# Another order inside the steps that ScalarE and VectorE interleave with a gated projection

## The chip, the cores and the metric

One core of one Trainium2 chip runs the whole program in one launch. The metric is the device time of a run in microseconds (us); lower is better. Three runs of the kernel before gave a median of 799.67 us (799.30 to 800.97).

## The reference

Attention with a window and sinks, then a gated projection, all in float32. There are 4 batches, 8 heads, 768 positions, head size 64. A query sees the first 4 positions (the sinks) and the 128 positions up to its own:

```python
scores = scale * np.matmul(q, k.transpose(0, 1, 3, 2))
keep = is_sink | in_window
scores = np.where(keep, scores, -1000000000.0)
a = softmax(scores)                 # row maximum taken off, 1e-9 added to the sum
x = np.matmul(a, v)                 # heads side by side: 3072 tokens x 512
out = ((x @ w_a) * (x @ w_b)) @ w_out   # 512 -> 1536 -> 512
```

## The kernel before, in words

The 3072 tokens are cut into 8 chunks of 2 to 4 tiles of 128 tokens (`CHUNKS`). `run` computes the projection of chunk c (`moe`) and, between its pieces, the attention of chunk c+1. The projection runs over 12 blocks j. A block is: `half("a", j)`, 12 matmuls into PSUM (L969); one step of attention; `half("b", j)`, 12 matmuls; a step; `project` of the block before, 9 matmuls of 512 columns (L978); a step. The text calls the three steps of a block A, B and O after the piece in front of them. Every product is kept in two rounded parts, high and low (`xh`, `xl`; `gh`, `gl`; hi and lo slots of `pt`).

The change touches the chunks whose attention is `steady`: chunks 3 to 7, computed during the projections of chunks 2 to 6. For those, `run` opens `manual_schedule` for TensorE, VectorE and ScalarE: these three engines execute in the order in which the program emits. GpSimd (POOL) and the DMA queue are ordered by the planner. Chunks 3 and 6 begin at tile 0 of their batch (below: head stages, during the projections of chunks 2 and 5); chunks 4, 5 and 7 begin at tile 3 (below: full stages, during the projections of chunks 3, 4 and 6).

A unit is one head and one tile of queries. `steady_plan` gives every step at most one unit to score, the unit scored two steps before to transpose, and at most one of three other things: `av` (the product of a head's three units with the values, three steps after its last unit), `skt` (transposes of four heads' sink weights) and `sk` (their product, twice). One step in the middle of the plan has no unit to score. In a step the operations are:

- scoring: two matmuls into the single PSUM tile `s` (L617); VectorE merges window edges and sinks (L625), subtracts and takes the maximum (L627); ScalarE exponentiates (L632); VectorE inverts the sum (L635, L636); ScalarE scales the unit (L642) and writes its sinks into `sc` (L645).
- turning a unit that lies wholly in the window ("joined"): a transpose into one half of the PSUM bank `t` (L661); ScalarE rounds it in place and into `p` (L674, L675); VectorE multiplies by a triangle and subtracts (L681, L682, L683) into `pt`, of which there is one.
- `av`: seven matmuls (L697); ScalarE copies one half of the rows (L704), VectorE adds the other (L707, L708).
- `skt`: three transposes into the tile tag `s` (L715); ScalarE rounds (L721), VectorE subtracts (L724), ScalarE copies both parts (L725). `sk`: one matmul (L731), VectorE adds (L733).
- the gate: ScalarE copies the a half to `g` (L988; one buffer); VectorE multiplies by the b half (L994); ScalarE rounds to `gh` (L999); GpSimd subtracts to `gl` (L1001), on VectorE in the last two blocks.

Before the change ScalarE's order in a step was: L988 (emitted in `moe` ahead of step A), L674, L675, L632, then `late_act` (L999, in step B), L704, L642, L645. VectorE's was: L994 (emitted in `moe` ahead of step B), L625, L627, L681 to L683, L635, L636, L707, L708. `between` spreads the steps over the blocks, about one after every piece.

Of the kernel before, what the change touches and what calls it, by code (L numbers as in the profile page):

```python
# [13 lines left out]
ALU = mybir.AluOpType  # L14
# [9 lines left out]
NJ = FF // P  # L24
# [199 lines left out]
class Fast:  # L224
# [367 lines left out]
    def steady(self, b, t0, nt, xf):  # L592
        nc = self.nc
# [6 lines left out]
        units = [(h, i) for h in range(H) for i in range(nt)]  # L600
        preps, state, sc, vss, skt, bank = {}, {}, {}, {}, {}, []

        def do_prep(h):
            if h < H:
                preps[h] = *self.prep_kq(b, h, t0, nt), self.prep_v(b, h, t0, nt)
                if h % 4 == 0:
                    vss[h // 4] = self.vs
# [125 lines left out]
            return (lambda: None), (lambda: V.tensor_tensor(x, ps[:, :cols], x, op=ALU.add))  # L733

        plan = self.steady_plan(units, nt)
        do_prep(0)
        yield
        for score, turn, rest in plan:
            turned = evicted = ()
            scored = ()  # L740
            if score is not None:
                if score[1] == 0:
                    do_prep(score[0] + 1)
                scored = scores(*score)
            if turn is not None:
                turned = transposes(*turn)
            if rest is not None:
                evicted = {"av": av, "skt": sinks_t, "sk": sinks_av}[rest[0]](*rest[1:])
            if turned:
                turned[0]()  # L750
            if scored:
                scored[0]()
                scored[1]()
            if turned:
                turned[1]()
            self.late_act()
            if evicted:
                evicted[0]()
            if scored:
                scored[2]()  # L760
                scored[3]()
            if evicted:
                evicted[1]()
            yield

    def steady_plan(self, units, nt):

        gap = 4 * nt + 1
        at = {}
        for k, u in enumerate(units):  # L770
            at[u] = k + (k >= gap)
        rest = {}
        for h in range(H):
            rest[at[h, nt - 1] + 3] = ("av", h)
        for g in range(2):
            k = at[4 * g + 3, nt - 1] + 2
            rest[k] = ("skt", g)
            for pr in range(2):
                while k in rest or k <= at[4 * g + 3, nt - 1] + 4:
                    k += 1  # L780
                rest[k] = ("sk", g, pr)
        score = {k: u for u, k in at.items()}
        turn = {k + 2: u for u, k in at.items()}
        n = max(*rest, *turn) + 1
        return [(score.get(k), turn.get(k), rest.get(k)) for k in range(n)]
# [169 lines left out]
    def moe(self, row, nt, xf, between, weights_ahead, last, weights_split, given):  # L955
        nc = self.nc
        n = nt * P
        tag = f"{row}"
        xs = self.split_x(xf, nt, tag)
        outs = [self.ps.tile([P, DM], F32, tag=("o0", "o1", "o2", "av")[i], name=f"o{tag}_{i}") for i in range(nt)]  # L960

        def half(kind, j):
            wh, wl = self.weight(kind, j)
            ps = self.ps.tile([P, 4 * P], F32, tag=kind, name=f"{kind}{tag}_{j}")
            for kk in range(NK):
                ksl = slice(kk * P, (kk + 1) * P)
                xh, xl = xs[kk]
                for i, (w, x) in enumerate(((wh, xh), (wh, xl), (wl, xh))):
                    nc.tensor.matmul(ps[:, :n], lhsT=w[:, ksl], rhs=x[:, :n],  # L969
                                     start=kk == 0 and i == 0, stop=kk == NK - 1 and i == 2)  # L970
            return ps

        def project(j, gh, gl):
            wh, wl = self.weight("o", j)
            for i in range(nt):
                sl = slice(i * P, (i + 1) * P)
                for k, (g, w) in enumerate(((gh, wh), (gh, wl), (gl, wh))):
                    nc.tensor.matmul(outs[i], lhsT=g[:, sl], rhs=w,  # L978
                                     start=j == 0 and k == 0, stop=j == NJ - 1 and k == 2)

        prev = None
        for j in range(NJ):
            if last and j == NJ - 2:
                self.ok = self.verdict(self.ps.tile([1, P], F32, tag="s", name="gp"))
            weights_ahead(3 * j)
            pa = half("a", j)
            g = self.mo.tile([P, max(n, 3 * P)], F32, tag="g", name=f"g{tag}_{j}", bufs=1)
            nc.scalar.copy(g[:, :n], pa[:, :n])  # L988
            between(3 * j)
            if last and j == NJ - 1:  # L990
                self.tc.mark_branch_hint_location("general", hint="LikelyTaken", engines=mybir.ALL_ENGINES)
            weights_ahead(3 * j + 1)
            pb = half("b", j)
            nc.vector.tensor_tensor(g[:, :n], pb[:, :n], g[:, :n], op=ALU.mult)  # L994
            gh = self.mo.tile([P, max(n, 3 * P)], F32R, tag="gh", name=f"gh{tag}_{j}")
            gl = self.mo.tile([P, max(n, 3 * P)], F32R, tag="gl", name=f"gl{tag}_{j}")

            def parts(j=j, g=g, gh=gh, gl=gl):
                nc.scalar.copy(gh[:, :n], g[:, :n])  # L999
                e = nc.gpsimd if weights_split and j < NJ - 2 else nc.vector  # L1000
                e.tensor_tensor(gl[:, :n], g[:, :n], gh[:, :n].bitcast(F32), op=ALU.subtract)  # L1001

            self.later.append(parts)
            if not given or j == NJ - 1:
                self.late_act()
            between(3 * j + 1)
            self.late_act()
            weights_ahead(3 * j + 2)
            if prev is not None:
                project(*prev)  # L1010
            between(3 * j + 2)
            prev = (j, gh, gl)
        project(*prev)
        for i in range(nt):
            r = row + i * P
            o = self.mo.tile([P, DM], F32, tag=("gh", "gl")[i % 2], name=f"os{tag}_{i}")
            (nc.vector.tensor_copy if last and i == 1 else nc.scalar.copy)(o, outs[i])
            (nc.sync if last else nc.scalar).dma_start(self.out[r:r + P, :], o)
# [175 lines left out]
```

## Time and profile before

| | |
|---|---|
| median of 3 runs | 799.67 us (799.30 to 800.97) |
| the profiled execution's own time | 800.83 us |
| its span, first to last instruction | 799.1 us |
| TensorE (PE) busy, weight loads (PEld) | 774.2 us (97%), 686.3 us (86%) |
| VectorE (DVE), ScalarE (ACT), GpSimd (POOL) busy | 525.0, 475.4, 292.2 us |
| granted TensorE clock | 0.996 of full speed |

The five steady stages lie between 242 us and 714 us of the span. Busy shares say who has most to do; how much time TensorE loses is read from the starts of its matmuls, because they are pipelined and the recorded end of one lies past the start of the next.

### The profile page before, as it was taken

The page shows a single profiled execution, that of the slowest core. Times are in us where ns is not written, and L with a number is a line of the kernel's source. Part 1 is how long each engine was busy: PE and PEld are TensorE (multiplying, and loading weights), DVE is VectorE, ACT ScalarE, POOL GpSimd, SP SyncE. Part 2 cuts the span into 40 slices and gives each one's busy share as a digit, 9 for nine tenths or more (in the row PEclk, how much of TensorE's full clock was granted, in tenths as well). Part 3 has the DMA queues.
Part 4 walks back from the last instruction along what each step waited for, and adds up shares of the span by engine and source line. Part 5 has one row for each costly group of instructions (what it writes and reads, how often), then busy time and mean ns, then how long its engine had stood idle before and what let it go on. Part 6 is the DMA issues. An engine that isn't in the chain of part 4 may idle for free.

```text
span 799.1 us, 13885 instructions
## 1 busy us (share of the span) xinstructions
PE 774.2 (97%) x4349; PEld 686.3 (86%) x4349; DVE 525.0 (66%) x1759; ACT 475.4 (59%) x1485; POOL 292.2 (37%) x400
## 2 busy tenths in 40 slices
PE   8999999989999999999999999999999999999997
PEld 5768777779799989998989889899998988889996
DVE  6888889977773767367873777636675487742321
ACT  5867577737755767366653666547774566644431
POOL 1110000146642655355660657406545375201110
PEclk9999999999999999999999999999999999999999
DMA  8777400242121332412111111212333121105511
GB/s 318 272 268 274 180 17 1 74 140 57 50 75 41 103 117 91 140 30 62 46 57 50 45 44 48 57 40 90 119 114 101 53 65 40 41 17 186 177 57 43
DMA packets 44574, 75.85 MB, mean 95 GB/s; under 512 B 4592, under 2 KB 24016, under 8 KB 44496
## 3 DMA queue, kind: packets, MB, share of 16 engines
q1 hardware_dynamic: 41440, 69.40, 27.0%
q10 hardware_dynamic: 3024, 5.51, 1.8%
q8 instruction: 36, 0.59, 0.3%
q14 instruction: 42, 0.34, 0.1%
q0 software_dynamic: 32, 0.00, 0.0%
HBM read 68.60 MB, written 6.29 MB: 94 GB/s over the span
## 4 chain that ended last, share of the span: by engine, by line
PE 59%; DVE 23%; ACT 10%; issue 3%; POOL 2%; DMA 2%; ACTq 0%; DVEq 0%; POOLq 0%
PE a L969 16%; PE o L978 16%; PE b L969 14%; DVE pt L681 3%; DVE pt L683 3%; DVE t L682 2%; PE av L697 2%; PE s L831 2%; PE s L617 2%; ACT p L675 2%; ACT g L988 1%; PE av L885 1%; ACT p L642 1%; DVE st L636 1%; ACT sc L645 1%
## 5 line engine op out<-in xcount | busy, mean ns | idle before, releaser
L969 PE MATMUL a<-xh,w 128*128 128x384 f32 (+2 forms) x768 | 214.2, 342 | 0.8 <-ACT w L353 0.8
L969 PE MATMUL b<-xh,w 128*128 128x384 f32 (+2 forms) x768 | 213.9, 342 | 0.0
L978 PE MATMUL o<-w,gh 128*128 128x512 f32 x576 | 185.3, 402 | 1.0 <-ACT gh L999 1.0
L969 PEld LDWEIGHTS a<-xh,w 128*128 128x128 f32 x768 | 138.5, 188 | 5.9 <-ACT w L353 1.1
L969 PEld LDWEIGHTS b<-xh,w 128*128 128x128 f32 x768 | 138.8, 188 | 4.1 <-issue 0.3
L1001 POOL TENSOR_TENSOR gl<-g,gh 128x384 fp32r<-128x384 f32 x60 | 60.9, 1016 | 217.1 <-ACT gh L999 212.3
L969 PE MATMUL b<-xl,w 128*128 128x384 f32 (+2 forms) x384 | 129.3, 337 | 0.0
L969 PE MATMUL a<-xl,w 128*128 128x384 f32 (+2 forms) x384 | 129.0, 336 | 0.0
L994 DVE TENSOR_TENSOR g<-b,g 128x384 f32<-128x384 f32 (+2 forms) x96 | 53.2, 554 | 106.9 <-PE b L969 95.2
L978 PEld LDWEIGHTS o<-w,gh 128*128 128x128 f32 x576 | 103.5, 189 | 20.3 <-ACT gh L999 1.7
L978 PE MATMUL o<-w,gl 128*128 128x512 f32 x288 | 114.1, 397 | 0.4 <-DVE gl L1001 0.4
L988 ACT COPY g<-a 128x384 f32<-128x384 f32 (+2 forms) x96 | 45.5, 474 | 75.4 <-PE a L969 63.9
L969 PEld LDWEIGHTS a<-xl,w 128*128 128x128 f32 x384 | 72.3, 188 | 2.4
L969 PEld LDWEIGHTS b<-xl,w 128*128 128x128 f32 x384 | 72.4, 189 | 1.6
L999 ACT CAST gh<-g 128x384 fp32r<-128x384 f32 (+2 forms) x96 | 48.6, 506 | 36.4 <-DVE g L994 34.7
L642 ACT ACTIVATE p<-p,st 128x128 f32<-128x128 f32 x88 | 35.6, 405 | 58.2 <-DVE st L636 57.7
L387 POOL TENSOR_SCALAR ks<-kr 64x400 fp32r<-64x400 f32 (+1 forms) x48 | 29.0, 605 | 107.4 <-DVE pt L548 105.5
L632 ACT ACTIVATE p<-p,st 128x136 f32<-128x136 f32 (+2 forms) x120 | 51.2, 426 | 26.0 <-DVE st L627 24.5
L978 PEld LDWEIGHTS o<-w,gl 128*128 128x128 f32 x288 | 54.1, 188 | 14.3 <-DVE gl L1001 1.7
L390 POOL TENSOR_TENSOR ks<-kr,ks 64x400 fp32r<-64x400 f32 (+1 forms) x48 | 58.0, 1208 | 3.8
L681 DVE TENSOR_TENSOR pt<-t,tri 128x256 fp32r<-128x256 f32 x88 | 37.3, 424 | 33.0 <-ACT p L675 30.3
L387 POOL TENSOR_SCALAR qh<-qr 128x384 fp32r<-128x384 f32 x48 | 25.1, 523 | 69.7 <-PE s L617 41.0
(192 smaller groups left out, 1437.1 us busy)
## 6 DMA issues: line engine op xcount, KB each, us to landing
qr<-in_qT_dram SPq DMA_DIRECT2D x48, 192.0 KB, 2.4
raw<-in_wa_dram SPq DMA_DIRECT2D x12, 512.0 KB, 6.6
raw<-in_wb_dram SPq DMA_DIRECT2D x12, 512.0 KB, 6.9
raw<-in_wo_dram SPq DMA_DIRECT2D x12, 512.0 KB, 7.2
chk_a<-in_wa_dram SPq DMA_DIRECT2D x24, 256.0 KB, 2.9
chk_b<-in_wb_dram SPq DMA_DIRECT2D x24, 256.0 KB, 2.8
chk_o<-in_wo_dram SPq DMA_DIRECT2D x24, 256.0 KB, 2.8
out_dram<-os ACTq DMA_DIRECT2D x21, 256.0 KB, 2.0
```

Source lines behind the costliest of these rows:

```text
L387: self.nc.gpsimd.tensor_scalar(o, i, 1.0, 1.0, op0=ALU.mult, op1=ALU.mult)
L390: (self.nc.vector if self.no_gpsimd else self.nc.gpsimd).tensor_tensor(o, i, high.bitcast(F32), op=ALU.subtract)
L632: A.activation(p[:, :n], p[:, :n], AF.Exp, bias=st[:, 0:1], scale=-1.0, accum_out=st[:, 1:2])
L642: A.mul(p[:, NS:KB], p[:, NS:KB], st[:, 3:4])
L681: V.tensor_tensor(hs, tp[:, 1:2, :].broadcast_to([P, 2, P]), tri, op=ALU.mult)
L683: V.tensor_tensor(ls, tp[:, 0:1, :].broadcast_to([P, 2, P]), tri, op=ALU.mult)
L969: nc.tensor.matmul(ps[:, :n], lhsT=w[:, ksl], rhs=x[:, :n], start=kk == 0 and i == 0, stop=kk == NK - 1 and i == 2)
L978: nc.tensor.matmul(outs[i], lhsT=g[:, sl], rhs=w, start=j == 0 and k == 0, stop=j == NJ - 1 and k == 2)
L988: nc.scalar.copy(g[:, :n], pa[:, :n])
L994: nc.vector.tensor_tensor(g[:, :n], pb[:, :n], g[:, :n], op=ALU.mult)
L999: nc.scalar.copy(gh[:, :n], g[:, :n])
L1001: e.tensor_tensor(gl[:, :n], g[:, :n], gh[:, :n].bitcast(F32), op=ALU.subtract)
```

## The change

In `steady`: the sinks' transposes and their reading (L715, L721, L724, L725) come first in their step; ScalarE rounds the transposed unit before it exponentiates, as before, but `av`'s copy and add now come before the scaling; the unit scaled (L642, L645) is the one scored a step earlier; the inverse comes after; `late_act` comes last. In `moe`, the copy L988 becomes part of `late_act`, and so does the product L994, ahead of L999. In `steady_plan`, the `sk` products may follow the last `av` directly at the end, so the plan has 30 steps in place of 31, and `between` leaves out one more place (after the projection in block 5); all later steps of the plan come one place later, and the last one falls in the same place as before.

```diff
--- before.py
+++ after.py
@@ -733,35 +733,43 @@
             return (lambda: None), (lambda: V.tensor_tensor(x, ps[:, :cols], x, op=ALU.add))
 
         plan = self.steady_plan(units, nt)
+        pending = lambda: None
         do_prep(0)
         yield
         for score, turn, rest in plan:
-            turned = evicted = ()
-            scored = ()
+            turned = evicted = scored = ()
+            sinks = rest is not None and rest[0] == "skt"
             if score is not None:
                 if score[1] == 0:
                     do_prep(score[0] + 1)
                 scored = scores(*score)
+            if sinks:
+                evicted = sinks_t(rest[1])
+                evicted[0]()
+                evicted[1]()
             if turn is not None:
                 turned = transposes(*turn)
-            if rest is not None:
-                evicted = {"av": av, "skt": sinks_t, "sk": sinks_av}[rest[0]](*rest[1:])
+            if rest is not None and not sinks:
+                evicted = {"av": av, "sk": sinks_av}[rest[0]](*rest[1:])
+            if scored:
+                scored[0]()
             if turned:
                 turned[0]()
             if scored:
-                scored[0]()
                 scored[1]()
             if turned:
                 turned[1]()
-            self.late_act()
-            if evicted:
+            if evicted and not sinks:
                 evicted[0]()
+                evicted[1]()
+            pending()
+            pending = lambda: None
             if scored:
                 scored[2]()
-                scored[3]()
-            if evicted:
-                evicted[1]()
+                pending = scored[3]
+            self.late_act()
             yield
+        pending()
 
     def steady_plan(self, units, nt):
 
@@ -776,7 +784,7 @@
             k = at[4 * g + 3, nt - 1] + 2
             rest[k] = ("skt", g)
             for pr in range(2):
-                while k in rest or k <= at[4 * g + 3, nt - 1] + 4:
+                while k in rest or k - 1 in rest and rest[k - 1][0] == "av" and k + 1 < len(units):
                     k += 1
                 rest[k] = ("sk", g, pr)
         score = {k: u for u, k in at.items()}
@@ -985,17 +993,20 @@
             weights_ahead(3 * j)
             pa = half("a", j)
             g = self.mo.tile([P, max(n, 3 * P)], F32, tag="g", name=f"g{tag}_{j}", bufs=1)
-            nc.scalar.copy(g[:, :n], pa[:, :n])
+            self.later.append(lambda g=g, pa=pa: nc.scalar.copy(g[:, :n], pa[:, :n]))
+            if not given or j == NJ - 1:
+                self.late_act()
             between(3 * j)
+            self.late_act()
             if last and j == NJ - 1:
                 self.tc.mark_branch_hint_location("general", hint="LikelyTaken", engines=mybir.ALL_ENGINES)
             weights_ahead(3 * j + 1)
             pb = half("b", j)
-            nc.vector.tensor_tensor(g[:, :n], pb[:, :n], g[:, :n], op=ALU.mult)
             gh = self.mo.tile([P, max(n, 3 * P)], F32R, tag="gh", name=f"gh{tag}_{j}")
             gl = self.mo.tile([P, max(n, 3 * P)], F32R, tag="gl", name=f"gl{tag}_{j}")
 
-            def parts(j=j, g=g, gh=gh, gl=gl):
+            def parts(j=j, g=g, gh=gh, gl=gl, pb=pb):
+                nc.vector.tensor_tensor(g[:, :n], pb[:, :n], g[:, :n], op=ALU.mult)
                 nc.scalar.copy(gh[:, :n], g[:, :n])
                 e = nc.gpsimd if weights_split and j < NJ - 2 else nc.vector
                 e.tensor_tensor(gl[:, :n], g[:, :n], gh[:, :n].bitcast(F32), op=ALU.subtract)
```

## Rows read from the trace of the kernel before

**Rows 1.** Busy time of each engine in the five steady stages, in order (the stage of 242.3 and that of 525.5 are the head stages): the stretch in us, its length, then busy us and count of instructions of PE, PEld, DVE, ACT, POOL; PEclk, DMA share, GB/s.
```profile
242.30:332.10 89.80, 89.18 (x516) 83.21 (x516) 54.23 (x203) 57.23 (x192) 45.56 (x62) 1.00 0.32 100
332.10:429.00 96.90, 94.33 (x536) 86.55 (x535) 65.06 (x234) 55.61 (x188) 49.05 (x62) 1.00 0.17 51
429.00:525.50 96.50, 93.93 (x534) 86.17 (x533) 64.67 (x232) 55.22 (x188) 47.88 (x62) 1.00 0.17 48
525.50:617.00 91.50, 90.77 (x524) 84.55 (x523) 54.41 (x204) 58.09 (x192) 45.52 (x62) 1.00 0.33 101
617.00:713.70 96.70, 94.10 (x536) 86.31 (x535) 64.93 (x234) 55.39 (x188) 38.77 (x48) 1.00 0.14 41
```

**Rows 2.** What TensorE waited for in one full stage (332.1 to 429 us): waiting instruction, releaser, us in total, times, longest.
```profile
PE t L661 <- DVE st L635: 1.0, 3, 0.4
PE s L617 <- DVE sct L724: 0.8, 1, 0.8
PE t L661 <- DVE pt L683: 0.5, 1, 0.5
PE sk L731 <- DVE xf L733: 0.2, 1, 0.2
```

**Rows 3.** TensorE in order of time, one block of that stage, the pieces of the projection left out: start us, us, engine, line, operation, out<-in, count, idle time before and its releaser. The t rows are the transposes of steps A, B, O and the next A.
```profile
358.86 0.28 PE L617 MATMUL s<-ks,ql 128*128 128x264 f32 x1
358.98 0.27 PE L661 MATMUL t<-ident,p 128*128 128x128 f32 x1
...
361.30 0.29 PE L617 MATMUL s<-ks,ql 128*128 128x264 f32 x1
361.82 0.30 PE L661 MATMUL t<-ident,p 128*128 128x128 f32 x1 [0.23 <-DVE st L635]
361.88 1.02 PE L697 MATMUL av<-pt,vv 128*128 128x256 f32 x7
362.73 0.68 PE L978 MATMUL o<-w,gh 128*128 128x512 f32 x2
...
365.12 0.27 PE L661 MATMUL t<-ident,p 128*128 128x128 f32 x1
...
367.55 0.28 PE L661 MATMUL t<-ident,p 128*128 128x128 f32 x1
```

**Rows 4.** VectorE over the same block, same columns.
```profile
360.46 0.42 DVE L681 TENSOR_TENSOR pt<-t,tri 128x256 fp32r<-128x256 f32 x1 [0.64 <-ACT p L675]
...
361.25 0.42 DVE L683 TENSOR_TENSOR pt<-t,tri 128x256 fp32r<-128x256 f32 x1
361.59 0.14 DVE L635 TENSOR_SCALAR st<-st 128x1 f32<-128x1 f32 x1
...
361.85 0.56 DVE L994 TENSOR_TENSOR g<-b,g 128x384 f32<-128x384 f32 x1
...
363.12 0.42 DVE L681 TENSOR_TENSOR pt<-t,tri 128x256 fp32r<-128x256 f32 x1 [0.16 <-ACT p L675]
...
364.69 0.56 DVE L707 TENSOR_TENSOR xf<-av,xf 64x384 f32<-64x384 f32 x1
365.29 0.29 DVE L708 TENSOR_TENSOR xf<-av,xf 64x128 f32<-64x128 f32 x1
```

**Rows 5.** ScalarE over the same block, same columns.
```profile
359.50 0.46 ACT L988 COPY g<-a 128x384 f32<-128x384 f32 x1
359.86 0.27 ACT L674 CAST t<-t 128x128 fp32r<-128x128 f32 x1
...
362.82 0.27 ACT L675 CAST p<-t 128x128 fp32r<-128x128 f32 x1
...
363.40 0.50 ACT L999 CAST gh<-g 128x384 fp32r<-128x384 f32 x1
...
365.43 0.25 ACT L674 CAST t<-t 128x128 fp32r<-128x128 f32 x1
365.71 0.27 ACT L675 CAST p<-t 128x128 fp32r<-128x128 f32 x1
```

**Rows 6.** The first reading of the sinks in that stage (step A of block 5): TensorE, ScalarE and VectorE, same columns.
```profile
376.25 0.49 PE L715 MATMUL skt<-ident,sc 128*32 128x128 f32 x3
...
377.64 0.47 ACT L721 CAST sct<-skt 32x384 fp32r<-32x384 f32 x1
...
379.03 0.55 DVE L724 TENSOR_TENSOR sct<-skt,sct 32x384 fp32r<-32x384 f32 x1
...
379.61 0.51 ACT L725 CAST sct<-sct 64x384 fp32r<-64x384 f32 x1 [1.50 <-DVE sct L724]
```

**Rows 7.** ScalarE and VectorE near the end of that stage, same columns: the rounding of the gate followed at once by the second reading of the sinks, and a gate product followed by its rounding with both engines otherwise idle.
```profile
414.88 0.52 ACT L999 CAST gh<-g 128x384 fp32r<-128x384 f32 x1
415.29 0.47 ACT L721 CAST sct<-skt 32x384 fp32r<-32x384 f32 x1
...
421.92 0.56 DVE L994 TENSOR_TENSOR g<-b,g 128x384 f32<-128x384 f32 x1 [2.90 <-PE b L969]
...
422.51 0.52 ACT L999 CAST gh<-g 128x384 fp32r<-128x384 f32 x1 [2.21 <-DVE g L994]
```

**Rows 8.** GpSimd over a block with `av` in step B, same columns: the first instruction of a head's preparation and the gate's low part behind it.
```profile
370.13 0.51 POOL L387 TENSOR_SCALAR qh<-qr 128x384 fp32r<-128x384 f32 x1 [2.71 <-PE s L617]
...
375.15 1.02 POOL L1001 TENSOR_TENSOR gl<-g,gh 128x384 fp32r<-128x384 f32 x1
```

## The prediction

> **What bounds the kernel now.** I read the busy times by stage first [rows 1]. In the full stages TensorE is busy for 94.3 of 96.9 us and VectorE for 65; in the head stages TensorE has 0.6 to 0.7 us left. So TensorE sets the pace, and a change of order can win back only what TensorE waits. Who makes it wait [rows 2]: the transposes of the units and, once, a score behind the sinks' reading, 2.5 us of idle in a full stage. The recorded idle is too small: a score matmul is followed by its transpose after 0.12 us when nothing waits (358.86 to 358.98), and in step B of the block shown after 0.52 us (361.30 to 361.82) [rows 3]. That is 0.40 us lost where the row says 0.23. Some ten waits of a full stage, each 0.2 us more than its idle, make about 4.5 us, and the last sinks' product 0.2 more: 4.7 us a full stage, 14 us in three. That is the whole prize there.
>
> Where the waits come from: the transpose of step B starts 0.15 us after L683 of step A has ended (361.25 + 0.42) [rows 3, 4]. So a transpose waits until VectorE has finished the unit before it, although that one lies in the other half of the bank `t`. L683 was late because L681 waited 0.64 us for ScalarE [rows 4], which had done the copy of the gate (0.36 us from its start to that of L674) and, before it, the scaling [rows 5]. The change takes both out of the way of L674. It also puts something else there.
>
> **Part 1, the gate at the end of step B.** L994 used to run early in the step. Now it comes after the inverse, L999 waits for it, and on ScalarE the next step's L674 stands behind L999. I count from the start of step B's transpose to the earliest start of the next step A's. Transpose to L674 0.31 (365.12 to 365.43) [rows 3, 5]; L674 to L675 0.28 [rows 5]; L675 to L681 0.30 (362.82 to 363.12) [rows 4, 5]; L681 to L683 0.79 and L683 to L635 0.34 [rows 4]; L635 to L994 0.26 [rows 4]; L994 and the step to L999 0.59 (421.92 to 422.51) [rows 7]; L999 to the next ScalarE instruction 0.41 (414.88 to 415.29) [rows 7]; then L674, L675 and L681 to L683 of step O again, 0.28 + 0.30 + 0.79; L683's length 0.42 and 0.15 to the transpose. Sum 5.22 us. TensorE's own way from step B to the next A without `av` is 2.45 (the transpose's 0.06, then 362.73 to 365.12) and 2.43 (365.12 to 367.55): 4.88 us [rows 3]. It will wait 0.34 us in such a step A. With `av` in step B, L681 waits for `av`'s reading of `pt` (it ends 1.08 us after the transpose [rows 3], of which I take 1.04, as the slots written first are read first), 0.15 more than above, and L707 and L708 stand ahead of the inverse: 0.60 and 0.25 [rows 4]. 6.22 against TensorE's own 5.73 (361.82 to 367.55) [rows 3]: 0.49 us.
>
> L999 to L674 has no row of its own. Its ends are 0.36 us, as after the copy L988 [rows 5], and 0.50 us, L999's whole length [rows 5]; I take 0.41, the one row of L999 with a cast from PSUM behind it [rows 7]. The Trainium skill, "ScalarE: Activation LUTs", section "What ACT_TABLE_LOAD costs", says that ScalarE instructions issued back to back overlap by about 93 ns. By that rule L999's 0.50 us would leave 0.41 and the wait is the one above; without any overlap each step A would wait 0.09 us longer, some 0.5 us more per full stage.
>
> **Part 2, the scaling a step later.** It costs nothing on any path: L642 and L645 now run behind L632, without waiting for the inverse, half a microsecond or more ahead of the transpose that needs them. The wait of L642 goes; what is late next is L999. Between step A and B the transpose to L683 and on takes 0.31 + 0.28 + 0.30 + 0.79 + 0.42 + 0.15 = 2.25 us [rows 3 to 5], and TensorE needs 2.43: no wait is left there.
>
> **Part 3, the sinks' reading first.** In step A of block 5, from the first sink transpose: 0.49 to the end of the third and 0.03 [rows 6], L721 0.47 and 0.03, L724 0.55 and 0.03 [rows 6], L725 to L674 0.41 (no row; between 0.36 and its 0.51), then 0.28 + 0.30 + 0.79 + 0.42 + 0.15 to the next transpose: 3.95 us. TensorE's own way is 0.25 for the three, 0.06, and 2.43: 2.74. It waits 1.2 us; before, the score behind L724 waited about 1.1. At the end the second reading now stands in step O of block 9, behind L999: from step B's transpose L681 0.89, L994 at 2.02, L999 at 2.61, L721 at 3.02, L724 3.52, L725 4.10, L674 4.51, L683 5.88 to 6.30, and the `av` product that needs it at 6.40. TensorE gets there, after the projection, the sinks and the a half, at 5.07. It waits 1.3 us, where the old order had put the projection over L683 and waited for nothing. The cover that is lost is that projection.
>
> **Part 4, the plan.** One step fewer and a place left out after block 5's projection change no work. The late `av` fall into step A, which leaves step B without them. Around the first `sk` I leave the 0.7 us of before: VectorE's add now stands ahead of the inverse and in the gate's chain, while the bank is free earlier. The last `sk` gains 0.2. DMA issues stay where they are in their steps; the later heads' preparation and loads come one place later, and their queues hold nothing that TensorE waits for in rows 2.
>
> **Sum for a full stage.** Step A of blocks 2, 8 and 9: 3 × 0.34; of 3 and 4: 2 × 0.49; block 5: 1.2; around `sk` 0.7; last `av` 1.3. Together 5.2 us, against 4.7 before: +0.5, three times +1.5. The head stages have two thirds of their units outside L681 to L683 and only 0.6 to 0.7 us of idle [rows 1]; their sinks are one tile of three, so I put -0.2 for each, between -0.7 (all idle gone) and +0.5 (Part 3 at a third). The other chunks keep their order. Sum +1.1 us. The profiled execution took 800.83 us, 1.73 over its span and 1.16 over the median; set on the median, 799.67 + 1.1 = **800.8 us**. Its own bounds: with 0.36 for L999 and L725, 0.05 less at eight places of each full stage, and the head stages at -0.7, 798.6; with no overlap behind L999, 0.1 more in six steps A of each, and +0.5 per head stage, 804.0.
>
> **The rivals.** *Faster: the gate's chain is hidden.* Place: step O of every block, L674 behind L999. If the chain from step B to the next A is 0.35 to 0.5 us shorter than my 5.22 and 6.22, because L994 gets done earlier or the links overlap, the waits of step A vanish: 2.0 us of the five and 0.4 of block 7's, 2.4 a full stage, 7.2 in three. 800.8 - 7.2 = 793.6. For it: the scaling's wait does go, and with it one of the two things that held L674. Against it: every link has a row, and they are in series. *Slower: GpSimd holds the gate.* `g` has one buffer, so L988 waits for L1001, and ScalarE's queue now stands behind L988 with the next L674 first. L999 will end 4.4 us after step B's transpose, L1001 5.4 if GpSimd is free, and L988's turn comes at about 7.9: 2.5 us in hand. It decides when more than that stands ahead of L1001: in the trace a head's preparation runs from 370.13 to 375.15 ahead of it [rows 8], 5.0 us. If all of that came behind L999, step B would start 2.5 us late, of which TensorE's slack takes 0.9; half of that, 0.8 us in the two blocks of a full stage where it meets `av`, is 4.8 us in three stages: 805.6. For it: the low part's start moves later by 2 us; against it, the preparation's first instruction waits for TensorE and starts long before L999. *Nothing happens:* the engines do not follow the written order. Rows 4 and 5 show them following it, so this has little.
>
> **How the numbers follow.** About 0.2% is what a measurement of this kernel can tell from no change: 1.6 us, 798.1 to 801.3. The forecast gets 0.52, of which 0.30 lies within that, 0.15 above and 0.07 below, as its bounds reach further up. The faster rival gets 0.24, the slower one 0.20, nothing 0.04. So faster 0.31, same 0.34, slower 0.35. The likeliest case alone spans 798.6 to 804.0; the range goes to both rivals' ends, 793.5 to 806.5, and leaves out about half of what each rival could exceed.
>
> **What would show it.** Right: in a full stage the transposes of step B no longer wait and those of step A wait 0.3 to 0.5 us, with L674 of step O starting at the end of L999; the last `av` waits over 1 us behind L683; L642 has no idle before it. The total of TensorE's waits is near 5 us a full stage. Wrong: step A's transpose runs straight after its score (the faster rival), or L988 has idle released by L1001 in blocks 2 to 9 (the slower one), or the head stages change by over 1 us.

## The result, and the profile after

The changed kernel takes 805.21 us, the median of 5 runs (804.81 to 806.96), against 799.67 us (799.18 to 800.97, 5 runs) before: ratio 1.0073, 95% interval 1.0058 to 1.0088. It is slower by 5.5 us, where +1.1 was forecast. The profiled execution took 805.09 us, its span is 803.4 us. That is 4.3 us over the span of the execution before and not 5.5: there the first steady stage begins at 243.29 us, here at 242.25, so about 1 us of the difference lies ahead of the stages. Lines of `moe` have moved: L969, L978, L988, L994, L999 and L1001 are now L977, L986, L996, L1009, L1010 and L1012; those of `steady` that the text uses are where they were.

Busy time by stage, from the first `a` matmul of a stage to that of the next (columns as in [rows 1]):

```profile
242.20:335.90 93.70, 92.52 (x529) 85.63 (x529) 54.94 (x205) 57.15 (x193) 45.42 (x62) 1.00 0.31 96
335.90:433.90 98.00, 94.20 (x535) 86.68 (x534) 64.94 (x232) 54.96 (x188) 49.10 (x62) 1.00 0.17 50
433.90:531.90 98.00, 94.20 (x535) 86.67 (x534) 64.94 (x232) 54.91 (x188) 47.92 (x62) 1.00 0.16 47
531.90:624.10 92.20, 91.07 (x523) 84.57 (x522) 54.00 (x202) 56.95 (x192) 45.42 (x62) 1.00 0.31 101
624.10:722.30 98.20, 94.40 (x536) 86.69 (x535) 65.50 (x234) 55.08 (x188) 38.77 (x48) 1.00 0.13 41
```

The engines do the same work as in [rows 1]: TensorE is busy for 94.2 us of a full stage again, and its granted clock is 1.00. The stages are longer. Cut by the same marks ([rows 1] cuts them 1 to 4 us earlier, so its lengths differ), they took 92.79, 96.70, 96.70, 91.45 and 96.84 us before and take 93.66, 98.02, 98.01, 92.20 and 98.12 us now: 1.3 us more in each full stage and 0.8 to 0.9 in each head stage, 5.5 together. So it is waiting that has grown.

Who makes TensorE wait in one full stage (335.9 to 433.9 us; columns as in [rows 2]):

```profile
PE t L661 <- DVE st L635: 1.7, 5, 0.7
PE t L661 <- DVE pt L683: 1.0, 2, 0.7
PE av L697 <- DVE pt L681: 0.4, 1, 0.4
PE av L697 <- DVE pt L683: 0.4, 1, 0.4
```

The score that waited for L724 is gone, and the transposes wait 2.7 us where [rows 2] had 1.5. L635 is only the instruction that ended nearest the transpose; what the transpose needs is L683, just ahead of it. Counted from starts of matmuls, as the prediction did, the waits are: steps A of blocks 2, 8 and 9, 0.34, 0.33 and 0.38 us; of blocks 3 and 4, 0.61 and 0.89; block 5, 1.34; around the first `sk`, 0.80; the last `av`, 1.29. Together 6.0 us, where the prediction had 5.2 and counted 4.7 before.

TensorE over blocks 3 and 4 of that stage, the projection left out (columns as in [rows 3]): the transposes of a step A (359.04), of the next block's step B (361.51) and of the step A behind that (368.12).

```profile
358.31 0.28 PE L617 MATMUL s<-ks,ql 128*128 128x264 f32 x1
359.04 0.30 PE L661 MATMUL t<-ident,p 128*128 128x128 f32 x1 [0.45 <-DVE st L635]
361.26 0.28 PE L617 MATMUL s<-ks,qh 128*128 128x264 f32 x1
361.38 0.29 PE L617 MATMUL s<-ks,ql 128*128 128x264 f32 x1
361.51 0.27 PE L661 MATMUL t<-ident,p 128*128 128x128 f32 x1
...
367.11 0.28 PE L617 MATMUL s<-ks,ql 128*128 128x264 f32 x1
368.12 0.30 PE L661 MATMUL t<-ident,p 128*128 128x128 f32 x1 [0.73 <-DVE st L635]
```

In [rows 3] it is the transpose of step B that waits, 0.52 us behind its score, and that of A runs at once. Now B runs 0.13 us behind its score and A comes 1.01 behind (367.11 to 368.12). VectorE and ScalarE between those two transposes:

```profile
362.55 0.43 DVE L681 TENSOR_TENSOR pt<-t,tri 128x256 fp32r<-128x256 f32 x1 [0.20 <-PE av L697]
363.01 0.30 DVE L682 TENSOR_TENSOR t<-t,p 128x128 f32<-128x128 f32 x1
363.41 0.42 DVE L683 TENSOR_TENSOR pt<-t,tri 128x256 fp32r<-128x256 f32 x1
363.87 0.56 DVE L707 TENSOR_TENSOR xf<-av,xf 64x384 f32<-64x384 f32 x1
364.46 0.29 DVE L708 TENSOR_TENSOR xf<-av,xf 64x128 f32<-64x128 f32 x1
364.77 0.15 DVE L635 TENSOR_SCALAR st<-st 128x1 f32<-128x1 f32 x1
364.96 0.16 DVE L636 RECIPROCAL st<-st 128x1 f32<-128x1 f32 x1
365.15 0.56 DVE L1009 TENSOR_TENSOR g<-b,g 128x384 f32<-128x384 f32 x1
...
367.55 0.42 DVE L683 TENSOR_TENSOR pt<-t,tri 128x256 fp32r<-128x256 f32 x1
```

```profile
365.75 0.51 ACT L1010 CAST gh<-g 128x384 fp32r<-128x384 f32 x1 [1.74 <-DVE g L1009]
366.17 0.26 ACT L674 CAST t<-t 128x128 fp32r<-128x128 f32 x1
```

This is the chain of Part 1, link for link: the product last on VectorE, ScalarE idle for 1.74 us until it ends, L674 straight behind L1010, and the transpose 0.15 us behind the second L683.

### The profile page after: what moved, and what is told of

The parts are those of the page before. It is cut to its first block, busy times and chain, and to the rows that moved or that the text cites. A ratio compares the mean times of both kernels' runs of the same rounds, so it can differ in the third digit from the quotient of the medians.

```text
span 803.4 us, 13683 instructions
## 1 busy us (share of the span) xinstructions
PE 774.1 (96%) x4349; PEld 686.3 (85%) x4349; DVE 524.1 (65%) x1759; ACT 471.1 (59%) x1485; POOL 292.0 (36%) x400
## 4 chain that ended last, share of the span: by engine, by line
PE 65%; DVE 20%; ACT 9%; issue 2%; POOL 2%; DMA 1%; DVEq 0%; POOLq 0%; ACTq 0%
PE b L977 19%; PE a L977 16%; PE o L986 16%; PE av L697 3%; DVE pt L681 3%; DVE pt L683 2%; PE s L617 2%; DVE t L682 2%; DVE g L1009 2%; ACT gh L1010 2%; PE s L839 2%; ACT p L675 1%; PE av L893 1%; ACT t L674 1%; PE t L661 1%
## 5 line engine op out<-in xcount | busy, mean ns | idle before, releaser
L977 PE MATMUL a<-xh,w 128*128 128x384 f32 (+2 forms) x768 | 215.1, 343 | 0.8 <-ACT w L353 0.8
L977 PE MATMUL b<-xh,w 128*128 128x384 f32 (+2 forms) x768 | 213.3, 341 | 0.0
L986 PE MATMUL o<-w,gh 128*128 128x512 f32 x576 | 185.2, 402 | 1.0 <-ACT gh L1010 1.0
L977 PEld LDWEIGHTS a<-xh,w 128*128 128x128 f32 x768 | 138.4, 188 | 6.4 <-ACT w L353 1.1
L977 PEld LDWEIGHTS b<-xh,w 128*128 128x128 f32 x768 | 139.4, 189 | 3.9 <-issue 0.3
L1012 POOL TENSOR_TENSOR gl<-g,gh 128x384 fp32r<-128x384 f32 x60 | 61.0, 1017 | 213.5 <-ACT gh L1010 212.4
L977 PE MATMUL b<-xl,w 128*128 128x384 f32 (+2 forms) x384 | 129.3, 337 | 0.0
L977 PE MATMUL a<-xl,w 128*128 128x384 f32 (+2 forms) x384 | 129.0, 336 | 0.0
L986 PEld LDWEIGHTS o<-w,gh 128*128 128x128 f32 x576 | 103.4, 188 | 20.2 <-ACT gh L1010 1.6
L986 PE MATMUL o<-w,gl 128*128 128x512 f32 x288 | 114.1, 397 | 0.3 <-DVE gl L1012 0.3
L1010 ACT CAST gh<-g 128x384 fp32r<-128x384 f32 (+2 forms) x96 | 49.2, 512 | 95.8 <-DVE g L1009 94.1
L1009 DVE TENSOR_TENSOR g<-b,g 128x384 f32<-128x384 f32 (+2 forms) x96 | 52.6, 548 | 60.0 <-PE b L977 53.8
L996 ACT COPY g<-a 128x384 f32<-128x384 f32 (+2 forms) x96 | 45.3, 472 | 52.4 <-PE a L977 50.2
L977 PEld LDWEIGHTS a<-xl,w 128*128 128x128 f32 x384 | 72.3, 188 | 2.7
L977 PEld LDWEIGHTS b<-xl,w 128*128 128x128 f32 x384 | 72.3, 188 | 1.6
L986 PEld LDWEIGHTS o<-w,gl 128*128 128x128 f32 x288 | 54.1, 188 | 14.3 <-DVE gl L1012 1.7
L681 DVE TENSOR_TENSOR pt<-t,tri 128x256 fp32r<-128x256 f32 x88 | 37.4, 425 | 37.4 <-ACT p L675 29.9
L390 POOL TENSOR_TENSOR ql<-qr,qh 128x384 fp32r<-128x384 f32 x48 | 49.0, 1022 | 2.2
```

Source lines behind the costliest of these rows:

```text
L390: (self.nc.vector if self.no_gpsimd else self.nc.gpsimd).tensor_tensor(o, i, high.bitcast(F32), op=ALU.subtract)
L681: V.tensor_tensor(hs, tp[:, 1:2, :].broadcast_to([P, 2, P]), tri, op=ALU.mult)
L977: nc.tensor.matmul(ps[:, :n], lhsT=w[:, ksl], rhs=x[:, :n], start=kk == 0 and i == 0, stop=kk == NK - 1 and i == 2)
L986: nc.tensor.matmul(outs[i], lhsT=g[:, sl], rhs=w, start=j == 0 and k == 0, stop=j == NJ - 1 and k == 2)
L996: self.later.append(lambda g=g, pa=pa: nc.scalar.copy(g[:, :n], pa[:, :n]))
```

## The experiments

Each row is one kernel: its median, the ratio to the kernel before on the same chip with its 95% interval, and the lengths of the five stages in the profiled execution (head, full, full, head, full), cut as above.

| kernel | us | ratio | stages, us |
|---|---|---|---|
| before | 799.67 | | 92.79, 96.70, 96.70, 91.45, 96.84 |
| changed | 805.21 | 1.0073 (1.0058 to 1.0088) | 93.66, 98.02, 98.01, 92.20, 98.12 |
| e1: product early | 792.50 | 0.9914 (0.9901 to 0.9928) | 92.66, 94.46, 94.47, 91.23, 94.57 |
| e2: sinks after | 801.45 | 1.0021 (1.0011 to 1.0030) | 92.95, 97.14, 97.52, 91.49, 97.26 |
| e3: old plan | 809.23 | 1.0122 (1.0107 to 1.0138) | 95.90, 96.62, 96.63, 96.33, 96.74 |
| e4: e1 and e2 | 788.72 | 0.9863 (0.9848 to 0.9878) | 92.56, 93.24, 93.27, 91.10, 93.36 |
| b1: before, scaling later | 797.25 | 0.9970 (0.9959 to 0.9981) | 94.81, 94.57, 94.57, 93.19, 94.65 |
| b2: before, gate late | 822.93 | 1.0295 (1.0275 to 1.0315) | 99.89, 101.15, 101.17, 95.83, 100.96 |
| e5: rounding behind L674 | 794.52 | 0.9934 (0.9920 to 0.9947) | 93.26, 94.62, 94.58, 91.55, 94.73 |
| e6: e4, copy early | 798.33 | 0.9982 (0.9973 to 0.9991) | 95.67, 94.37, 94.36, 93.95, 94.47 |
| e7: e4, scaling before sinks | 785.59 | 0.9828 (0.9815 to 0.9841) | 92.07, 92.61, 92.60, 90.57, 92.72 |
| e8: e4, old plan | 790.03 | 0.9876 (0.9861 to 0.9891) | 93.13, 93.10, 93.11, 91.45, 93.23 |

**e1, the product early.** The changed kernel, with the product back behind the b half:

```diff
             pb = half("b", j)
+            nc.vector.tensor_tensor(g[:, :n], pb[:, :n], g[:, :n], op=ALU.mult)
...
             def parts(j=j, g=g, gh=gh, gl=gl, pb=pb):
-                nc.vector.tensor_tensor(g[:, :n], pb[:, :n], g[:, :n], op=ALU.mult)
```

> The changed kernel with one thing put back: VectorE multiplies the gate's halves right behind the b half, ahead of step B's inverse; the roundings to gh and gl stay at the end of the step. Theory 1 (the gate's chain through the end of step B, into the next L674, is what TensorE waits for in steps A): the transposes of step A in blocks 2 to 4, 8 and 9, which wait 0.33 to 0.89 us in the changed kernel, stop waiting, and L674 of step O no longer stands behind a late L1010; about 2.5 to 3 us less in each full stage, 0.5 to 1 in each head stage: 792 to 797 us. Theory 2 (the sinks' reading first and the shorter plan cost the time, the gate only fills what would be idle anyway): within 1.5 us of 805.2.

Measured 792.50 us, 12.7 less than the changed kernel: 3.5 in each full stage, more than the 2.5 to 3 expected, and 1.0 in each head stage. Theory 1 holds. In the full stage the waits of steps A of blocks 2, 3, 4, 8 and 9 are gone; what is left is block 5 (1.21 us), a transpose of block 8 (0.30) and the last `av` (1.01).

**e2, the sinks' reading after the unit's.**

```diff
-            sinks = rest is not None and rest[0] == "skt"
+            sinks = False
...
-                evicted = {"av": av, "sk": sinks_av}[rest[0]](*rest[1:])
+                evicted = {"av": av, "skt": sinks_t, "sk": sinks_av}[rest[0]](*rest[1:])
```

> The changed kernel with the sinks' transposes and their reading back behind the unit's transpose and its reading (L721, L724, L725 after L683), all else as changed. Theory 1 (gate alone): block 5 and the last av are only where the waits happen to show, the total stays within 1 us of 805.2. Theory 2 (sinks): the last av's wait of 1.3 us goes in each full stage and 0.7 in each head stage, and block 5's 1.3 becomes the 1.1 of the kernel before: about 1.5 us less in each of three full stages and 0.5 in each of two head stages, 799.7; both can hold in part, the gate's share then is what stays above the kernel before in steps A.

Measured 801.45 us, 3.8 less than the changed kernel, between the two theories' figures and nearer the second. The last `av`'s wait is gone in the full stage; block 5's became 1.8 us, spread over three places (0.86, 0.33 and 0.61), instead of 1.1. The sinks are a term of their own, the smaller one.

**e3, the old plan.**

```diff
-                while k in rest or k - 1 in rest and rest[k - 1][0] == "av" and k + 1 < len(units):
+                while k in rest or k <= at[4 * g + 3, nt - 1] + 4:
```

> The changed kernel with the old rule for the places of the two sk products (31 steps, a place of the stage less left out), all else as changed. Theory 1 (gate): the late av fall back into other steps, so that the late steps A keep only their 0.3 us each; the total stays within 1.5 us of 805.2. Theory 2 (the plan put av and the last sinks where nothing covers them): the last av's wait and the waits of blocks 8 and 9 fall by about 1.2 us a full stage together: 801 us or less.

Measured 809.23 us: neither. The full stages are 1.4 us shorter, so the new plan's later `av` do cost what theory 2 said; the head stages are 2.2 and 4.1 us longer, which no theory had. Together that is 2.2 us of the 4.0 between the medians; the traced execution took 807.54 us, 1.7 below the median, and where the rest lies is not shown. The first head stage shows where the loss comes from. TensorE's projection waits for the gate's low part:

```profile
324.92 0.68 PE L986 MATMUL o<-w,gh 128*128 128x512 f32 x2
327.95 0.50 PE L986 MATMUL o<-w,gl 128*128 128x512 f32 x1 [2.35 <-POOL gl L1012]
```

ScalarE had rounded that gate at 320.80, but on GpSimd a head's preparation stands ahead of L1012:

```profile
322.13 0.74 POOL L390 TENSOR_TENSOR vv<-vr,vv 128x256 fp32r<-128x256 f32 x1
...
326.22 0.72 POOL L390 TENSOR_TENSOR vv<-vr,vv 128x256 fp32r<-128x256 f32 x1
326.90 0.99 POOL L1012 TENSOR_TENSOR gl<-g,gh 128x384 fp32r<-128x384 f32 x1
```

That is the mechanism of the rival in which GpSimd holds the gate, with another waiter (L986 in place of L996) and in the other stages. The changed kernel differs by the plan alone, which starts the preparations a place later, and its projections wait for GpSimd nowhere in the five stages. The second head stage of e3 has the same wait, 2.32 us at 615.97; it loses 1.9 us more than the first, and TensorE's clock fell behind it (last section).

**e4, e1 and e2 together** (both edits above).

> Both put back, the product of the gate early and the sinks' reading after the unit's; what stays of the change is the scaling one step later, the copy of the a half and the two roundings late, and the plan. If gate and sinks are separate terms that add up, the gain of the first kernel and that of the second add: 786 to 793 us, faster than the kernel before (799.7), since the wait of the scaling for the inverse is gone and nothing new holds L674. If they are one wait seen at two places, the time is that of the better of the two alone.

Measured 788.72 us, 16.5 less than the changed kernel: 12.7 + 3.8. By stage it is less tidy: the full stages lose 4.8 us where the parts give 3.5 and 0.5 to 0.9, the head stages 1.1 where they give 1.0 and 0.7, so in the head stages the two edits partly remove the same wait. It is 1.4% faster than the kernel before.

**b1, the scaling alone, on the kernel before.**

```diff
-                scored[3]()
+            pending()
+            pending = lambda: None
+            if scored:
+                pending = scored[3]
```

> The kernel before with one part of the change alone: L642 and L645 of a unit come one step later, ahead of the next inverse; gate, sinks and plan as before. Theory 1 (the scaling waits for the inverse and the next L674 stands behind it, so it is one of the two things that make the transposes of step B wait): the waits of 0.4 to 0.6 us in steps B of blocks 2 to 4 and those of 0.15 in steps A become smaller, 1 to 2 us less in a full stage: 794 to 797 us. Theory 2 (the copy of the a half in front of L674 is what holds; the scaling was hidden): within 1 us of 799.6.

Measured 797.25 us. Theory 1 holds in the full stages, with 2.1 to 2.2 us off each, just over its 1 to 2. But the head stages grow by 2.0 and 1.7 us, which neither theory had. There TensorE waits for the scaling itself:

```profile
262.42 0.50 ACT L1004 CAST gh<-g 128x384 fp32r<-128x384 f32 x1
262.94 0.48 ACT L704 COPY xf<-av 64x384 f32<-64x384 f32 x1
263.32 0.51 ACT L640 ACTIVATE p<-p,st 128x264 f32<-128x264 f32 x1
```

```profile
263.16 0.27 PE L617 MATMUL s<-ks,ql 128*128 128x128 f32 x1
263.88 0.44 PE L664 MATMUL t<-ident,p 128*128 128x128 f32 x2 [0.45 <-ACT p L640]
```

With `gh` (here L1004) and `av`'s copy ahead of it, a scaling that comes a step later ends 0.05 us before the transpose that needs it starts. In b1 `late_act` still stands ahead of the scaling, so this is not yet Part 2's order; but the changed kernel, too, has scalings in the head stages that end only 0.05 us before their transpose (the transpose at 273.96 us waits 0.17 us). Part 2 had them half a microsecond early.

**b2, the gate's part alone, on the kernel before:** the copy of the a half and the product are emitted as in the change, and

```diff
-            self.late_act()
             if evicted:
                 evicted[0]()
             if scored:
                 scored[2]()
                 scored[3]()
             if evicted:
                 evicted[1]()
+            self.late_act()
```

> The kernel before with the gate's part alone: the copy of the a half, the product, gh and gl at the end of their steps; scaling, sinks and plan as before. Theory 1 (the late gate is a loss by itself): product and rounding in front of the next L674 make steps A wait as in the changed kernel or more, since the scaling still stands ahead of them, 1 to 3 us more in a full stage; and with the old plan a head's preparation on GpSimd stands ahead of gl in the head stages, as in the changed kernel with the old plan, 3 to 5 us more in each: 808 to 816 us. Theory 2 (the gate is a loss only beside the new places of the sinks): 800 us or less, because the copy leaves L674's way.

Measured 822.93 us, 2.95% slower than before and above the upper end of theory 1. The full stages grow by 4.1 to 4.5 us: L642 waits up to 1.5 us for the inverse, and the copy and the rounding of the gate, and L674 after them, stand behind it. The head stages grow by 7.1 and 4.4; GpSimd holds a projection for 3.05 us in the first and 3.10 in the second, and in the first TensorE's clock fell behind the wait (last section). e3 has the same late gate and the same plan, with the scaling later and the sinks first, and takes 13.7 us less. The sinks first were no gain beside the late gate with the new plan (e2), so the later scaling probably makes the difference; a run with it alone beside the late gate was not made.

**e5, the rounding behind the next L674.** The product stays at the end of step B; L1010 and L1012 go into a list of their own, which `late_round` empties:

```diff
             if turned:
                 turned[0]()
+            self.late_round()
             if scored:
                 scored[1]()
```

> The changed kernel with the gate's product left at the end of step B, but its rounding (L1010, and L1012 behind it) emitted in the next step behind L674 and L675. It tells by which engine the late gate holds the transposes. By ScalarE (L674 and L675 stand behind L1010, which waits for the product): the waits of steps A go as with the early product, 2.5 to 3.5 us less in a full stage: 792 to 796 us. By VectorE (the product lies between the inverse and the next unit's L681): the waits stay, 804 to 806 us.

Measured 794.52 us, 10.7 less than the changed kernel. The full stages are within 0.2 us of e1's, so the product at the end of the step does no harm on VectorE; it is ScalarE's queue that carries the wait. ScalarE in block 4's step O (L1010 is L1018 here, L674 and L675 are L679 and L680):

```profile
363.73 0.25 ACT L679 CAST t<-t 128x128 fp32r<-128x128 f32 x1 [1.09 <-PE t L666]
364.01 0.27 ACT L680 CAST p<-t 128x128 fp32r<-128x128 f32 x1
364.38 0.52 ACT L1018 CAST gh<-g 128x384 fp32r<-128x384 f32 x1
```

L679 waits for its transpose alone, as it should. The head stages stay 0.6 and 0.3 us above e1's, and there the projection waits for `gl`, 1.3 us in two places: the low part now starts later.

**e6, e4 with the copy of the a half early.**

```diff
-            self.later.append(lambda g=g, pa=pa: nc.scalar.copy(g[:, :n], pa[:, :n]))
...
+            nc.scalar.copy(g[:, :n], pa[:, :n])
             between(3 * j)
-            self.late_act()
```

> The kernel with the product early and the sinks' reading after the unit's, with the copy of the a half also back ahead of step A, as before; of the change only the scaling one step later, the late rounding and the plan are left. If the copy in front of L674 was part of the loss of the kernel before: 0.1 to 0.36 us more in each step A, up to 2 us in a full stage: 790 to 796 us. If only the scaling had mattered there: within 1 us of 788.7.

Measured 798.33 us, 9.6 more than e4: 1.1 in each full stage, 2.9 to 3.1 in each head stage. Of the two parts taken out of e4 singly, the late copy pays far more than the plan (1.3, e8); the scaling was not taken out of e4. The total is 2 us above the first theory's range: its price in the full stages lies within what was expected, in the head stages it is above. There the copy, at the head of ScalarE's queue, waits for GpSimd to have read the last `g`. ScalarE's waits from 242 to 335 us, e6 and then e4:

```profile
ACT g L996 <- POOL gl L1009: 4.2, 3, 1.9
```

```profile
ACT g L996 <- POOL gl L1012: 0.8, 1, 0.8
```

The longest wait of TensorE in that stage is a new one, 1.5 us of idle at 327.84 before the `sk` product (L731), behind VectorE's L708. I haven't followed the rest of those 3 us link by link.

**e7, e4 with the scaling ahead of the sinks' reading.**

```diff
+            if rest is not None and rest[0] == "skt":
+                pending()
+                pending = lambda: None
             if evicted and not sinks:
                 evicted[0]()
                 evicted[1]()
```

> The fastest kernel so far (product early, sinks' reading after the unit's, 788.7) with one change: in the step with the sinks' transposes the scaling of the unit before comes ahead of the sinks' reading. There the transpose of block 5's step B still waits 0.61 us, by the trace for L642, which stands behind L725. If that row names the cause: 0.4 to 0.6 us less in each of three full stages, up to 0.4 in each head stage: 786.2 to 787.5 us. If the transpose is late for the copy L996 or L725 in front of L674 instead: within 0.6 us of 788.7.

Measured 785.59 us, 3.1 less than e4 and 0.6 below the expected range: 0.6 to 0.7 in each full stage and 0.5 in each head stage, each a little more than expected. The row of e4 named the cause rightly: its only wait of TensorE in a full stage (334.7 to 427.9 us), with the two ScalarE instructions that made it:

```profile
PE t L661 <- ACT p L642: 0.4, 1, 0.4
```

```profile
375.67 0.51 ACT L725 CAST sct<-sct 64x384 fp32r<-64x384 f32 x1 [1.50 <-DVE sct L724]
376.19 0.40 ACT L642 ACTIVATE p<-p,st 128x128 f32<-128x128 f32 x1
```

This is the fastest kernel of the study, 1.7% faster than before.

**e8, e4 with the old plan** (e3's edit on e4).

> The same fastest kernel with the old rule for the sk products (31 steps). In the changed kernel with that rule the head stages lost 2.2 and 4.1 us to GpSimd (a projection waited 2.4 us for gl, behind the preparation of a head). If the late product made gl late there, gl is in time here and the plan matters little: 787 to 790 us. If the order of the steps against the preparations makes it, whatever the product's place, the head stages lose the same: 793 to 796 us.

Measured 790.03 us, 1.3 more than e4, at the edge of the first theory's range; the two ratios' intervals overlap. The head stages lose 0.6 and 0.3 us where e3's lost 2.2 and 4.1, and the full stages gain 0.1 each. The five stages thus hold 0.5 us of the 1.3; in the profiled execution the rest lies ahead of them, as its first steady stage begins at 243.28 us and e4's at 242.15. So with the product in its old place the plan matters little: the wait of e3 needs both, a late product and a preparation ahead of `gl`. (e8 also has the sinks back in their place; b2 has them there too and waits, so they are not what removes it.)

## Why the prediction was right or wrong

**What bounds the kernel: right.** The change and every experiment move TensorE's waits; its busy time in the stages hardly moves.

**Part 1, the gate's chain: right in mechanism, too short in two blocks.** Every place named waits, and the step B transposes no longer do. Without `av` 0.34 us was forecast, and 0.34, 0.33 and 0.38 came. With `av` 0.49 was forecast, and 0.61 and 0.89 came. The links say where the rest lies. In block 4, by the rows above, L681 to L683 takes 0.86 us where 0.79 was counted, L683 to L707 0.46 instead of 0.34, L708 to L635 0.31 instead of 0.25, L635 to L1009 0.38 instead of 0.26: 0.37 us in four links, of a miss of 0.40 (0.89 - 0.49). In block 3 VectorE's part, L681 to L1009, takes the 2.24 us that were counted, and one link on ScalarE is long:

```profile
356.56 0.51 ACT L1010 CAST gh<-g 128x384 fp32r<-128x384 f32 x1 [1.47 <-DVE g L1009]
357.10 0.25 ACT L674 CAST t<-t 128x128 fp32r<-128x128 f32 x1
```

That is 0.54 us from L1010 to L674 where 0.41 was taken and block 4 has 0.42; that 0.13 is the miss (0.61 - 0.49 = 0.12). The prediction took each link's duration from one row, and that row happened to be a short one. Its upper bound for this one link, 0.50, was too low by 0.04. The Trainium skill, "ScalarE: Activation LUTs", section "What ACT_TABLE_LOAD costs", has an overlap of about 93 ns between ACTIVATEs issued back to back; the pair here are CASTs. Block 4's pair agrees with it (0.51 less 0.42 is 0.09) and block 3's has no overlap at all. e1 and e5 show the part as a whole: 12.7 us come off when the product is early, 10.7 when only the rounding is moved from in front of L674.

**Part 2, the scaling at no cost: wrong in two places.** The waits of L642 went, as said. In the step that follows, the first sinks' transpose needs the L645 which has just been put off. A head stage, ScalarE and TensorE:

```profile
281.89 0.29 ACT L645 ACTIVATE sc<-p,st 128x8 f32<-128x8 f32 x1
```

```profile
282.23 0.28 PE L715 MATMUL skt<-ident,sc 128*32 128x128 f32 x1 [0.32 <-ACT sc L645]
```

That makes 0.49 us in the head stage and 0.18 in the full one. And "half a microsecond or more ahead" holds in the full stages (0.6 us at least), but in the head stages the margin falls to 0.05 us, as said at b1. The wait for L645 is a meeting of Parts 2 and 3, which were costed apart; the scaling goes later by a step and its reader comes earlier within one.

**Part 3, the sinks first: right.** Block 5 waits 1.34 us (forecast 1.2), of which 0.18 is the wait just named. The last `av` waits 1.29 (forecast 1.3), 0.45 and 0.41 of it as recorded idle behind the second reading:

```profile
418.81 0.41 PE L697 MATMUL av<-pt,vv 128*128 128x256 f32 x2
419.66 0.38 PE L697 MATMUL av<-pt,vv 128*128 128x256 f32 x1 [0.45 <-DVE pt L681]
420.45 0.68 PE L697 MATMUL av<-pt,vv 128*128 128x256 f32 x4 [0.41 <-DVE pt L683]
```

**Part 4, the plan: sized wrongly by itself.** Around the first `sk` 0.80 us came (0.7 forecast), but the plan was not free: beside the late gate it costs 1.4 us a full stage and saves 2.2 to 4.1 a head stage (e3), an estimated 1.9 of the 4.1 by the clock. The net is a gain of 2.2 in the stages shown and 4.0 between the medians, which the forecast, looking at the steps alone, had as nothing.

**The step that failed: the head stages.** The sum gave them -0.2 us each, between -0.7 and +0.5, from the idle left to them and no chain. They came out at +0.87 and +0.75, outside those bounds, though below the 1 us at which the prediction called itself wrong. Four waits make most of it: 0.49 at the first sinks' transpose, 0.52 at the next transpose behind the sinks' reading, 0.41 in two later steps, 0.64 at the last `av`; before, the same count gives 1.4 us in all (0.55, 0.14, 0.33 and 0.34), so the 0.6 to 0.7 us of idle on which the forecast rested was too small a figure here as well. Part 3 at a third was too little a share: from the first sinks' transpose to L674 it is 1.13 us there (282.23 to 283.36) against 2.21 in the full stage (376.06 to 378.27), so about half; and e1 takes 1.0 us off each head stage, so the gate's chain reaches into them as well. The account closes: 0.8 us too little in each of three full stages and about 1.0 in each of two head stages is 4.4, and the miss is 5.5 - 1.1 = 4.4. The full stages' 0.8 are sizes rather than a path: 0.52 of it the links of Part 1 in blocks 3 and 4, the rest block 5 and the first `sk`.

**The rivals.** The faster one fell: the chain is longer than 5.22 and 6.22, not shorter. The slower one gave the right sign and nearly the time (805.6) for a reason that the trace does not show: ScalarE's waits for GpSimd at L996 are 0.3 us in all five stages.

```profile
ACT g L996 <- POOL gl L1012: 0.3, 2, 0.2
```

The likeliest case was bounded at 804.0, so the measured 805.2 lies inside the stated range only because that reaches to this rival's end. That is luck: what made the time is not what set the end. The rival's mechanism is real, as e3 and b2 show, and lay one plan away.

## What to carry to other kernels

A late piece of work costs by what is queued behind it: here the product could stay last on VectorE, as long as the ScalarE instruction that waits for it did not stand in front of the one that feeds TensorE (e5). A bundle of reorderings should be taken apart before it is dropped: this one lost 0.7%, and without two of its moves (the late product, the sinks first) it gains 1.4%, with one more swap 1.7%. Where several steps each move by a little, look for the pair in which a producer goes later and its reader earlier.

## What the runs showed of the hardware

Three pairs of instructions that follow each other start at one of two distances each. Over the five stages of the changed kernel, L1010 to L674 is 0.42 us in 19 of 27 cases and 0.54 to 0.55 in 8, with nothing between; L636 to L1009 is 0.08 in 35 and 0.19 to 0.20 in 10; L683 to L707, where no longer wait lies between, 0.34 in 12 and 0.46 in 9. The step is 0.11 to 0.12 us in all three, on both engines. I did not find what decides which; VectorE's part of the chain in block 4 came out 0.37 us longer than the rows that the prediction had taken.

In b2 the wait for GpSimd cost more than its own length. TensorE before, in and after the wait in the first head stage (columns as in [rows 1]):

```profile
325.00:329.50 4.50, 1.84 (x11) 1.41 (x9) 0.29 (x1) 0.00 (x0) 4.16 (x7) 0.96 0.25 68
329.50:334.00 4.50, 4.11 (x11) 3.44 (x12) 1.41 (x3) 1.72 (x6) 0.34 (x1) 0.50 0.61 191
334.00:339.00 5.00, 5.00 (x25) 4.96 (x24) 1.15 (x3) 2.15 (x5) 0.00 (x0) 0.80 0.00 0
```

After 3.05 us without a matmul the granted clock was 0.50, the lower of its two levels, from 329.5 to 334 us, and back at 1.00 in the stretch from 339 on. After the 3.10 us of the second head stage it stayed at 1.00:

```profile
630.50:633.00 2.50, 2.19 (x10) 1.88 (x11) 1.01 (x2) 1.73 (x6) 0.25 (x1) 1.00 0.65 164
```

In e3 it was the other way round. After the 2.35 us of idle shown above, the clock stayed at 1.00 from 328 to 333 us; after the 2.32 us of the second head stage it was 0.50 from 617 to 620:

```profile
617.00:620.00 3.00, 3.00 (x10) 2.70 (x9) 0.87 (x3) 0.66 (x3) 0.00 (x0) 0.50 0.52 160
```

So of four waits, two of about 3.1 and two of about 2.3 us, one of each length brought the lower clock and one did not: in these runs the length of the wait alone does not say which. By the difference between the two head stages of one execution, the fall cost an estimated 2.7 us in b2 (7.1 - 4.4) and 1.9 in e3 (4.1 - 2.2). A wait of this kind has to be read together with the clock of the stretch behind it.
